# Spectral filter and leaky feed-forward in one kernel: first layer begun with two token groups, 8-byte runs from the first transposes, and a new plan for the later batches

## The chip, the cores and the metric

The kernel runs on one core of one Trainium2 chip. The metric is the device time of one execution in microseconds (us). Before the change four executions took 754.4 to 758.41 us, with a median of 756.79. Lower is better.

## The reference

The input `x` holds 8 batches of 3008 tokens of 256 features. Along the tokens of each batch a real Fourier transform is taken, multiplied with a complex filter, and transformed back. Then every one of the 24064 tokens goes through two matrix products with a leaky ReLU between them.

```python
X = np.fft.rfft(x, axis=1)                       # x: (8, 3008, 256)
Y = X * (filt_r + 1j * filt_i)[None, :, :]
y = np.fft.irfft(Y, n=3008, axis=1)
h = y.reshape(24064, 256) @ w_in                 # 256 -> 2048
out = np.maximum(0.01 * h, h) @ w_out            # 2048 -> 256, float32
```

## The kernel before, in words

**The transform.** 3008 is 94 times 32, so a transform of one batch is four small matrix stages with a turn of the layout between the first and the second pair. For a batch `b` these are: `s1` (line 219, 16 groups of one matmul, over the 94), `s2` (line 265, 12 groups of two matmuls, over the 32), the filter, `sa` (line 285, 12 groups of one matmul, back over the 32), and `sb` (line 303, 16 groups of four matmuls, back over the 94), which writes the tokens' features into `yt`. A group of `s1` fills one PSUM bank and is copied to SBUF by VectorE (DVE) or ScalarE (ACT), line 222. Two groups together are stored to a DRAM buffer `dz1` (line 224, 256 KB) and, when all eight stores have landed, read back turned, six reads of 256 KB, of which `z1` holds four (line 229). `sa` does the same through `dz2` and `z2`: stores at line 289, reads at line 234, copies at line 287.

**The filter.** For one `s2` group DVE multiplies the bank with the two parts of the filter (lines 274 and 277; for the even groups of batch 1 the exchange of real and imaginary halves is done by two half-width multiplications, lines 271 and 272). For the others two DMAs (lines 275, 276) exchange the halves in SBUF. GpSimd (POOL) adds (line 279); the sum is what `sa` reads.

**Batch 0** takes another way, without DRAM: `first_s1`, four DVE transposes (line 255), `first_s2` (line 328; ACT copies at line 336 and POOL multiplications at line 339 take some of its groups), `first_sa` (line 349), four more DVE transposes (line 357), and `first_sb` (line 366, 16 groups of eight matmuls, groups 0 to 7 for the first 128 features and 8 to 15 for the last 128; each group is copied to `yt` at line 295). Nothing of the feed-forward runs before all 16 are issued.

**The feed-forward** works on 47 chunks of 512 tokens. `moe1` (line 442, 32 matmuls of 512 columns for a chunk, more where a chunk crosses two batches) fills pairs of banks `ph`, which ACT takes through the leaky ReLU (line 447, 1024 columns at a time). The second product of chunks 0 to 3 and of the last is plain (line 545, 64 matmuls of 256 columns; results are copied at line 550). For the chunks between, seven half-size products (line 493, 112 matmuls of 128 columns) stand for eight; they need four sums of 2048 columns on DVE (line 470, `act_sums`), and one DVE or ACT instruction that takes each product out of its bank (lines 517 to 537).

**The order** is written by hand. A heap `work` holds closures with a planned time; they are run in order of time, and what they call is recorded in that order on each engine's queue. Each engine then works through its own queue strictly in order, held only by semaphores. The planned unit is an eighth of a chunk: chunk `ci` of `moe1` is spread over times 8 ci to 8 ci + 8, its second product over the eight units after that. `plan(b, ...)` gives each batch a start and a step for `s1`, `s2`, `sa` and `sb`; two groups are never nearer than `GAP` = 0.6 units. Planned times decide the order only.

All DMAs of `dz1`, `dz2`, the exchange and the output are issued by SyncE (SP), from one queue: an issue that waits for its data holds up all issues behind it. The loads of `x` are issued by POOL.

**Banks.** Until the first layer begins the transform stages use three single banks `pf` and two double ones `ph`. From there two `pf` banks are left for `s1`, `s2`, `sa` and `sb` in turn, and the third and `po_ps` serve the second product.

The lines that set the order around the change, before:

```python
t1_part(0, 0, True)(), t1_part(0, 1, True)()            # 390, writes flat
for g in range(8, 16):                                  # 420
    first_sb(g, act if g in (10, 12, 14) else dve, two[(g // 2) % 2])
plan(1, 0.3, 0.55, 12.8, 1.25, 3.3, 37, 2.8, 4, 1.6)    # 575
plan(2, 13, 1.55, 43.5, 2.6, 5.5, 84.2, 2.8, 13, 2.3)
plan(3, 42, 1.75, 75, 3.75, 6, 129, 2.94, 4, 2.94)
after = when[stage, b, 15 if stage == 1 else 11] + LANDED      # 591
at(max(time, after, place.get((stage, c % 4), 0)), f)
```

Of the kernel before, what the change touches and what calls it, by code (L numbers as in the profile page):

```python
# [73 lines left out]
def kernel(  # L74
# [25 lines left out]
    LANDED = 1.7  # L100
    SUMS = (0.9, 1.9, 2.9, 3.9)
# [45 lines left out]
    def at(time, f):  # L147
        clock["n"] += 1
        heapq.heappush(work, (time, clock["n"], f))

# [63 lines left out]
    st1, st2, st1_more = ring(big[2], 0), ring(big[2], 1), ring(big[0], 0)  # L214

    def s1_group(b, g, copy):
        def go():
            ps = bank("pf", 2, D)
            nc.tensor.matmul(ps, fwd1[:N1], x_sb[:N1, ds(2 * g, 2), :], start=True, stop=True)  # L219
            h = g // 2  # L220
            st = st1[h % 4] if b > 1 or h < 4 else st1_more[h % 4]
            copy(st[:, ds(2 * (g % 2), 2), :], ps)  # L222
            if g % 2:
                soon(0.7, lambda: nc.sync.dma_start(dz1[b % 2][ds(4 * h, 4)].rearrange("n p d -> p n d"), st))
        return go

    def t1_load(b, c):
        def go():
            nc.sync.dma_start(z1[c % 4], turned(dz1[b % 2], N2, c))
        return go  # L230

    def t2_load(b, h):
        def go():
            nc.sync.dma_start(z2[h % 4][:K4], turned(dz2[b % 2], NC, h))
        return go
# [11 lines left out]
    def t1_part(b, i, flat=False):  # L247
        def go():
            a = big[(4 * b) % 3][:].bitcast(FP32)[:, ts(i, E4 * Q)].rearrange("p (e n) -> p e n", n=Q)
            o = big[(4 * b + 1) % 3][:].bitcast(FP32)  # L250
            if flat:
                o = o[:, ts(i, E4 * Q)].rearrange("p (e n) -> p e n", n=Q)
            else:
                o = o.rearrange("p (n e) -> p e n", n=Q)[:, ts(i, E4), :]
            nc.vector.transpose(o, a)
        return go


    ys = {}

    def s2_group(b, g):
        def go():
            ps = bank("pf", 2, D)
            for j in range(2):
                nc.tensor.matmul(ps[:, j, :], f2_sb[:, 2 * g + j, :],  # L265
                                 z1[g // 2 % 4][:, 2 * (g % 2) + j, :],
                                 start=True, stop=True)
            fa, fb = fa_sb[:, ds(2 * g, 2), :], fb_sb[:, ds(2 * g, 2), :]
            p1, p2, p3 = (scrp.tile([P, 2, D], FP32, tag=f"p{i}", name=f"p{i}_b{b}_g{g}") for i in (1, 2, 3))
            if b == 1 and g % 2 == EXG:  # L270
                nc.vector.tensor_tensor(p3[0:64], ps[64:P], fb[64:P], AL.mult)
                nc.vector.tensor_tensor(p3[64:P], ps[0:64], fb[0:64], AL.mult)
            else:
                nc.vector.tensor_tensor(p2[:], ps, fb, AL.mult)  # L274
                soon(1, lambda: nc.sync.dma_start(p3[0:64], p2[64:P]))
                soon(1, lambda: nc.sync.dma_start(p3[64:P], p2[0:64]))
            nc.vector.tensor_tensor(p1[:], ps, fa, AL.mult)  # L277
            ys[(b, g)] = y1 = ypp.tile([P, 2, D], FP16, tag="y", name=f"y_b{b}_g{g}")
            soon(1.2 if b == 1 and g % 2 == EXG else 3 if b > 1 else 2.6, lambda: nc.gpsimd.tensor_tensor(y1[:], p1[:], p3[:], AL.add))  # L279
        return go  # L280

    def sa_group(b, g):
        def go():
            ps = bank("pf", 2, D)
            nc.tensor.matmul(ps, inv2, ys.pop((b, g))[:], start=True, stop=True)  # L285
            h = g // 2
            nc.scalar.copy(st2[h % 4][:, ds(2 * (g % 2), 2), :], ps)  # L287
            if g % 2:
                soon(0.7, lambda: nc.sync.dma_start(dz2[b % 2][ds(4 * h, 4)].rearrange("k p d -> p k d"), st2[h % 4]))
        return go  # L290
# [6 lines left out]
    def sb_group(b, g, copy):  # L297
        h, dt = g // 2, g % 2

        def go():  # L300
            ps = bank("pf", 4, N1)
            for j in range(4):
# [21 lines left out]
    def first_s2(hf, c, n, kind, on_pool=False):  # L324
        ps = bank(kind, n, DH)
        src = paired(big[1])
        for j in range(n):
            nc.tensor.matmul(ps[:, j, :].rearrange("p (e t) -> p e t", t=2), f2_sb[:, c + j, :],
                             src[:, c + j, ts(hf, DH // 2)], start=True, stop=True)
# [29 lines left out]
    def first_sb(g, copy, kind):  # L359
        dt, h = g // 8, g % 8  # L360
        src = big[0][:].rearrange("p (h n e r t) -> p h n r t e", h=2, n=Q // 2, r=2, t=2)
# [28 lines left out]
    t1_part(0, 0, True)(), t1_part(0, 1, True)()  # L390
    upper(0, fa_sb, act), upper(0, fb_sb, minus)
    first_s2(0, 8, 8, "ph", True)
    t1_part(0, 2, True)()
# [7 lines left out]
    t1_part(0, 3, True)()  # L401
# [18 lines left out]
    for g in range(8, 16):  # L420
        first_sb(g, act if g in (10, 12, 14) else dve, two[(g // 2) % 2])
# [44 lines left out]
    def act_sums(ci, step):  # L466
# [3 lines left out]
        nc.vector.tensor_tensor(o, i0, i1, op)  # L470

# [15 lines left out]
    def product(ci, a, w, after):  # L487
# [4 lines left out]
        def one(t, c):  # L492
            nc.tensor.matmul(po[:, t], a()[:, c, ts(t, P)], w[:, c, :],  # L493
# [21 lines left out]
    def last_product(ci):  # L515
        def after(po):
            add(rows(ci, 0)[:, :, 1], po, rows(ci, 1)[:, :, 2], AL.add)
            soon(0.5, lambda: stores(ci, 0))
        return product(ci, lambda: s4, b22, after)

    def products(ci):
        a11, a12, a21, a22 = (lambda i=i, j=j: quarter(ci, i, j) for i in range(2) for j in range(2))

        def after5(po):
            add(rows(ci, 1)[:, :, 1:3], twice(po), part[1], AL.add)
            soon(0.5, lambda: stores(ci, 1))
# [8 lines left out]
        items += product(ci, a21, wt[2], lambda po: add(v7, po, t1, AL.add))  # L535
        items += product(ci, lambda: s2, wt[1], lambda po: add(part[1], twice(po), part[0], AL.add))
        items += product(ci, a22, wt[3], lambda po: add(rows(ci, 1)[:, :, 0], po, u3, AL.add))
        items += product(ci, lambda: s1, wt[0], after5)
        return items

    def plain(ci):

        def one(tj, ct):
# [7 lines left out]
            soon(0.5, lambda: store(ci, tj, ot[:]))  # L551
        return [lambda tj=tj, ct=ct: one(tj, ct) for tj in range(4) for ct in range(NCT)]

    groups, loads = [], []

    def plan(b, s1, s1_step, s2, s2_step, lag, sb, sb_step, xl, x_step):
        for g in range(16):
            groups.append((s1 + s1_step * g, 1, b, g, s1_group(b, g, dve if b == 1 and g % 4 < 3 else act)))
            if g % 2 and b + 1 < B:
                at(s1 + xl + x_step * g, lambda n0=2 * g - 2: x_load(b + 1, n0, 4))  # L560
        for c in range(6):
            loads.append((s2 - 3, 1, b, c, t1_load(b, c)))
# [3 lines left out]
        for h in range(8):  # L566
            loads.append((sb - 3, 3, b, h, t2_load(b, h)))
        for g in range(16):
            due = SL * (QT * (8 * b + g // 2) // CH)
            groups.append((min(sb + sb_step * g, due - 3.5 + 2 * (g % 2)), 4, b, g, sb_group(b, g, act)))  # L570
# [3 lines left out]
    at(26, lambda: nc.sync.dma_start(i1_sb[:K4], i1t_d.ap()))  # L574
    plan(1, 0.3, 0.55, 12.8, 1.25, 3.3, 37, 2.8, 4, 1.6)
    plan(2, 13, 1.55, 43.5, 2.6, 5.5, 84.2, 2.8, 13, 2.3)
    plan(3, 42, 1.75, 75, 3.75, 6, 129, 2.94, 4, 2.94)
    for b in range(4, B):
        z = 47 * b
        plan(b, z - 121, 2.94, z - 69, 3.92, 6.5, z - 11.6, 2.94, 4, 2.94)  # L580

    last, when = -1, {}
    for time, stage, b, g, f in sorted(groups, key=lambda v: v[0]):
        last = max(time, last + GAP)
        when[stage, b, g] = last
        at(last, f)
        assert stage < 4 or last < SL * (QT * (8 * b + g // 2) // CH), (b, g, last)
    place = {}
    for time, stage, b, c, f in loads:

        after = when[stage, b, 15 if stage == 1 else 11] + LANDED
        at(max(time, after, place.get((stage, c % 4), 0)), f)
        place[stage, c % 4] = when[stage + 1, b, 2 * c + 1] + 0.1
# [49 lines left out]
```

## Time and profile before

| What | Value |
|---|---|
| four executions | 756.01, 757.56, 754.4, 758.41 us |
| the profiled execution | 756.01 us, of which its span is 754.2 us |
| TensorE (PE) busy | 739.3 us, 98% of the span |
| ACT, DVE, POOL busy | 562.4, 484.6, 165.1 us |
| granted TensorE clock | 1.00 in every stretch of 20 us but the last (0.99) |
| first matmul of the feed-forward | 38.16 us |
| start of the last merged row of matmuls (16 of 256 columns) | 748.93 us |
| bytes moved by DMA | 113.29 MB, 150 GB/s on average |

Times in the profile count from the start of the span. A row of the timeline merges equal instructions that follow each other: its start, its length, the engine, the line, the operation, the tiles, partitions and columns, the count, and in brackets the idle time before it with what ended it. Matmuls are pipelined and their ends are modelled, so a row's length is longer than the time for which it holds PE; the distance from the start of one row to the start of the next is what the next one really waited.

### The profile page before, as it was taken

The page shows a single profiled execution, that of the slowest core. Times are in us where ns is not written, and L with a number is a line of the kernel's source. Part 1 is how long each engine was busy: PE and PEld are TensorE (multiplying, and loading weights), DVE is VectorE, ACT ScalarE, POOL GpSimd, SP SyncE. Part 2 cuts the span into 40 slices and gives each one's busy share as a digit, 9 for nine tenths or more (in the row PEclk, how much of TensorE's full clock was granted, in tenths as well). Part 3 has the DMA queues.
Part 4 walks back from the last instruction along what each step waited for, and adds up shares of the span by engine and source line. Part 5 has one row for each costly group of instructions (what it writes and reads, how often), then busy time and mean ns, then how long its engine had stood idle before and what let it go on. Part 6 is the DMA issues. An engine that isn't in the chain of part 4 may idle for free.

```text
span 754.2 us, 18976 instructions
## 1 busy us (share of the span) xinstructions
PE 739.3 (98%) x7829; PEld 529.1 (70%) x7829; DVE 484.6 (64%) x658; ACT 562.4 (75%) x755; POOL 165.1 (22%) x171
## 2 busy tenths in 40 slices
PE   8899999999999999999999999999999999999998
PEld 4555657667777777877678767787777777777776
DVE  5965525777666785667666756676677676555462
ACT  4876777788778877777778777878777777776663
POOL 4702421332222122221223222213111210000000
PEclk9999999999999999999999999999999999999999
DMA  9997786887875667555765656553554433111012
GB/s 189 247 208 200 171 203 179 195 197 204 224 205 147 142 189 203 149 154 129 209 173 143 170 135 181 147 142 115 149 161 116 118 96 104 53 64 54 29 44 70
DMA packets 119687, 113.29 MB, mean 150 GB/s; under 512 B 16352, under 2 KB 92768, under 8 KB 119408
## 3 DMA queue, kind: packets, MB, share of 16 engines
q1 hardware_dynamic: 104736, 95.59, 42.3%
q0 software_dynamic: 14864, 16.49, 15.4%
q8 instruction: 61, 1.00, 0.6%
q14 instruction: 26, 0.21, 0.1%
HBM read 57.48 MB, written 50.33 MB: 143 GB/s over the span
## 4 chain that ended last, share of the span: by engine, by line
PE 83%; DMA 3%; DVE 1%; ACT 0%; issue 0%; POOL 0%; SPq 0%; DVEq 0%; POOLq 0%; ACTq 0%
PE ph L442 38%; PE pf L493 17%; PE po_ps L493 17%; PE pf L303 3%; PE pf L219 2%; PE pf L285 2%; PE pf L265 2%; DMA big<-dz 1%; PE pf L545 1%; PE po_ps L545 1%; DMA p_b_g<-p_b_g 1%; DVE big L470 1%; DMA dz<-big 1%; DVE p_b_g L277 0%; POOL y_b_g L279 0%
## 5 line engine op out<-in xcount | busy, mean ns | idle before, releaser
L447 ACT ACTIVATE gt_c<-ph 128x1024 f16<-128x1024 f32 x376 | 385.1, 1024 | 138.0 <-PE ph L442 129.2
L442 PE MATMUL ph<-yt,w_in_sb 128*128 128x512 f16 (+7 forms) x1728 | 447.2, 351 | 0.1
L493 PEld LDWEIGHTS <-gt_c 128*128 128x128 f16 x2688 | 194.3, 98 | 89.5 <-issue 0.7
L279 POOL TENSOR_TENSOR y_b_g<-p_b_g,p_b_g 128x512 f16<-128x512 f32 x84 | 114.1, 1360 | 442.3 <-DMA p_b_g<-p_b_g 327.5
L493 PEld LDWEIGHTS <-big 128*128 128x128 f16 x2016 | 144.8, 98 | 62.2 <-issue 1.4
L442 PEld LDWEIGHTS <-w_in_sb 128*128 128x128 f16 x1728 | 138.1, 98 | 19.5 <-issue 0.8
L274 DVE TENSOR_TENSOR p_b_g<-pf,fb_sb 128x512 f32<-128x512 f32 x78 | 53.8, 690 | 50.6 <-PE pf L265 32.3
L222 ACT CAST big<-pf 128x512 f16<-128x512 f32 x100 | 58.2, 583 | 13.5 <-PE pf L219 12.4
L493 PE MATMUL pf<-wt_sb,gt_c 128*128 128x128 f16 x672 | 67.5, 219 | 0.0
L493 PE MATMUL po_ps<-wt_sb,gt_c 128*128 128x128 f16 x672 | 67.4, 219 | 0.0
L493 PE MATMUL po_ps<-wt_sb,big 128*128 128x128 f16 x672 | 64.8, 219 | 0.0
L493 PE MATMUL pf<-wt_sb,big 128*128 128x128 f16 x672 | 64.0, 219 | 0.0
L493 PE MATMUL po_ps<-w_out_sb,gt_c 128*128 128x128 f16 x672 | 64.0, 219 | 0.0
L493 PE MATMUL pf<-w_out_sb,gt_c 128*128 128x128 f16 x672 | 63.5, 219 | 0.1
L295 ACT CAST yt<-pf 128x376 f16<-128x376 f32 x117 | 55.1, 473 | 8.6 <-PE pf L303 6.0
L277 DVE TENSOR_TENSOR p_b_g<-pf,fa_sb 128x512 f32<-128x512 f32 x84 | 57.3, 682 | 0.2
L470 DVE TENSOR_TENSOR gt_c<-gt_c 128x2048 f16<-128x2048 f16 x42 | 54.5, 1297 | 1.1
L287 ACT CAST big<-pf 128x512 f16<-128x512 f32 x84 | 49.1, 584 | 8.1 <-PE pf L285 6.9
L470 DVE TENSOR_TENSOR big<-gt_c,big 128x2048 f16<-128x2048 f16 x42 | 54.6, 1300 | 0.0
L470 DVE TENSOR_TENSOR big<-gt_c 128x2048 f16<-128x2048 f16 x42 | 53.8, 1280 | 0.2 <-ACT gt_c L447 0.2
L470 DVE TENSOR_TENSOR big<-big,gt_c 128x2048 f16<-128x2048 f16 x42 | 53.3, 1269 | 0.0
L219 PE MATMUL pf<-x_sb,small_sb 94*128 94x512 f16 x112 | 42.7, 381 | 1.4 <-DVE p_b_g L277 1.3
(84 smaller groups left out, 640.2 us busy)
## 6 DMA issues: line engine op xcount, KB each, us to landing
dz<-big SPq DMA_DIRECT2D x98, 256.0 KB
p_b_g<-p_b_g SPq DMA_DIRECT2D x156, 128.0 KB
out_dram<-ost_c_h SPq DMA_DIRECT2D x114, 128.0 KB
big<-dz SPq DMA_DIRECT2D x42, 256.0 KB
big<-dz SPq DMA_DIRECT2D x56, 192.0 KB
x_sb<-in_x_dram POOLq DMA_DIRECT2D x41, 192.0 KB, 4.4
out_dram<-ost_c_t SPq DMA_DIRECT2D x14, 128.0 KB
x_sb<-in_x_dram POOLq DMA_DIRECT2D x2, 768.0 KB, 10.3
```

The source lines that it names most:

```text
L219: nc.tensor.matmul(ps, fwd1[:N1], x_sb[:N1, ds(2 * g, 2), :], start=True, stop=True)
L222: copy(st[:, ds(2 * (g % 2), 2), :], ps)
L274: nc.vector.tensor_tensor(p2[:], ps, fb, AL.mult)
L277: nc.vector.tensor_tensor(p1[:], ps, fa, AL.mult)
L279: soon(1.2 if b == 1 and g % 2 == EXG else 3 if b > 1 else 2.6, lambda: nc.gpsimd.tensor_tensor(y1[:], p1[:], p3[:], AL.add))
L287: nc.scalar.copy(st2[h % 4][:, ds(2 * (g % 2), 2), :], ps)
L295: copy(yv, ps.rearrange("p c a -> p a c"))
L303: nc.tensor.matmul(ps[:, j, :], z2[h % 4][:K4, j, ts(dt, P)], i1_sb[:K4, 4 * h + j, :], start=True, stop=True)
L442: nc.tensor.matmul(ph[:, j, ds(t - ci * CH, e - t)], w_in_sb[:, dt, ts(ct, P)], yt[:, dt, ds(t % N, e - t)], start=(dt == 0), stop=(dt == ...
L447: nc.scalar.activation(gts[ci][:, ds(2 * g, 2), :], ph, AF.Lrelu)
L470: nc.vector.tensor_tensor(o, i0, i1, op)
L493: nc.tensor.matmul(po[:, t], a()[:, c, ts(t, P)], w[:, c, :], start=(c == 0), stop=(c == NCH - 1))
```

## The change

- The first transposes write runs of 8 bytes: pairs of neighbouring `n` stand side by side, and `first_s2` reads them so (stride 8 bytes in place of 128).
- Only groups 0 to 9 of `first_sb` stand before the first layer. Groups 10 to 15 are put into the first layer's stream at the planned times `REST`, copied by ACT and DVE in turn.
- The second half of batch 1's staging moves from `big[0]` to `big[1]`, since `big[0]` is still read.
- `place` of a group: a group of `s2` or `sb` is planned no earlier than its read-back's issue, and a group of `sa` behind its POOL addition.
- All starts, steps and delays have new values, those of DVE's four sums (`SUMS`) too; a read-back is issued `LEAD` before its first use, where the stores allow it.

```diff
-    LANDED = 1.7
-    SUMS = (0.9, 1.9, 2.9, 3.9)
+    LANDED = 2.26
+    SUMS = (0.05, 1.51, 3.08, 4.47)
+    REST = (7.21, 11.38, 12.49, 9.32, 22.05, 21.68)
+    DUE = (3.63, 2.48)
+    LEAD = (3.88, 6.29)
+    AFTER = (0.72, 0.81, 2.69, 4.11, 0.05, 0.67)
+    PLANS = (
+        (0.68, 0.17, 11.96, 1.17, 4.08, 36.48, 2.68, 4.72, 1.5),
+        (11.42, 1.71, 43.45, 2.46, 6.81, 87.35, 2.71, 14.75, 1.96),
+        (39.96, 1.78, 73.73, 3.9, 6, 128.81, 2.82, 0.75, 2.65),
+        (63.05, 2.86, 119, 3.9, 7.12, 177.38, 3.11, 10.44, 2.21),
+    )
...
-    st1, st2, st1_more = ring(big[2], 0), ring(big[2], 1), ring(big[0], 0)
+    st1, st2, st1_more = ring(big[2], 0), ring(big[2], 1), ring(big[1], 1)
...
+    def first_t1(i):
+        a = big[0][:].bitcast(FP32)[:, ts(i, E4 * Q)].rearrange("p (e n r) -> p e n r", n=Q // 2, r=2)
+        o = big[1][:].bitcast(FP32).rearrange("p (n e r) -> p e n r", n=Q // 2, r=2)
+        nc.vector.transpose(o[:, ts(i, E4)], a)
+
+    def y_delay(b, g):
+        return 1.2 if b == 1 and g % 2 == EXG else AFTER[2] if b > 1 else AFTER[3]
...
-        src = paired(big[1])
+        src = big[1][:].rearrange("p (n e r t) -> p n r e t", n=Q // 2, r=2, t=2)
...
-    for g in range(8, 16):
-        first_sb(g, act if g in (10, 12, 14) else dve, two[(g // 2) % 2])
+    for g in (8, 9):
+        first_sb(g, (act, dve)[g % 2], "ph")
...
+    for g in range(10, 16):
+        at(REST[g - 10], lambda g=g: first_sb(g, (act, dve)[g % 2], "pf"))
...
+    def load_time(stage, b, c):
+        end = stage, b, 15 if stage == 1 else 11
+        if (stage, b, c) not in loads:
+            if end not in when or (c > 3 and (stage + 1, b, 2 * c - 7) not in when):
+                return None
+            loads[stage, b, c] = t = max(first_use[stage, b] - LEAD[stage // 2], place.get((stage, c % 4), 0),
+                                         when[end] + AFTER[4 * (stage // 2)] + LANDED)
+            at(t, (t1_load if stage == 1 else t2_load)(b, c))
+        return loads[stage, b, c]
...
+        if stage == 3:
+            behind = when[2, b, g] + y_delay(b, g) + 0.02 if (2, b, g) in when else None
+        else:
+            behind = load_time(stage - 1, b, g // 2) if stage != 1 else 0
+        if behind is None or behind + 0.02 > t:
+            heapq.heappush(queue, (t + GAP if behind is None else behind + 0.03, n, stage, b, g, f))
+            continue
+        when[stage, b, g] = last = t
+        at(t, f)
```

`AFTER` holds the delays from a copy to its `dz1` store, from the multiplication to the exchange, from it to POOL's addition (later batches, then the odd groups of batch 1), from a copy to its `dz2` store, and to an output store; before these were 0.7, 1, 3, 2.6, 0.7 and 0.5. `need` and `noted`, which the change also adds, only check the recorded order while the program is built. Batches 5 to 7 take the last line of `PLANS`, moved by 47 units each. The matmuls are the same before and after, 7829 of them; of the copies of `first_sb` one goes from DVE to ACT.

## The prediction

> **What bounds the kernel.** The first page says PE is busy for 739.3 of 754.2 us, but ends of matmuls are modelled, so I read PE's timeline from start to start. Back to back, a matmul of 512 columns holds PE for 0.216 us, one of 256 for 0.109, one of 128 for 0.056, one of `sb` for 0.045 (rows of 2 x 512 start 0.43 apart, 16 x 256 take 1.75, 16 x 128 0.89, 4 of `sb` 0.18). From the first matmul of the feed-forward (38.16) to the end of the last (748.93 + 1.75 = 750.7) are 712.5 us. The work in them is: `moe1` 1728 matmuls 325.3, the halved products 4704 x 0.056 = 263, plain ones 320 x 0.109 = 35, `s1` and `sa` 196 x 0.216 = 42.3, `s2` 168 x 0.109 = 18.4, `sb` 448 x 0.045 = 20.2; together 704.3. So PE sets the time, and some 8 us are waits. A change can win only these, and the start of the first layer. I then looked for each wait, as distance between starts less the work. Over 0.11 us they are: 1.75 at 56.9, 0.14 at 69.1, 0.33, 0.30, 0.30, 0.27, 0.17 between 74 and 100, 0.88 at 111.4, 1.47 at 142.1, 0.14 at 268.6, 0.58 at 365.3, 1.37 at 449.7, 0.12 at 499.8: **7.8 us**. Who ends them stands in the waits of PE (total, times, longest):
>
> ```profile
> PE pf L265 <- DMA big<-dz: 2.8, 2, 1.6
> PE ph L328 <- DVE big L255: 2.6, 2, 2.2
> PE pf L219 <- DVE p_b_g L277: 1.3, 1, 1.3
> ...
> PE pf L303 <- DMA big<-dz: 0.7, 1, 0.7
> ...
> PE pf L285 <- POOL y_b_g L279: 0.4, 1, 0.4
> ```
>
> Read-backs (L265, L303), one late filter product (L277), one late addition (L279). L328 lies in the prologue.
>
> **Start of the first layer.** Before, PE begins the second half of `first_sb` at 35.52, when the last transpose ends (33.09 + 2.37 = 35.46), and the first layer 2.64 later. After, only groups 8 and 9 stand there: two groups take PE 0.49 (rows of 16 start 0.49 apart). ACT's eight copies of groups 0 to 7 end at 35.46 + 0.92 = 36.38; group 8's (0.47) ends at 36.85, DVE copies group 9 beside it. So the first layer can start at 36.85: **-1.3**. The six groups come back as 48 matmuls x 0.031: **+1.5**.
>
> **First transposes.** The DVE rows L255 (flat, 1233 ns) and L357 (already 8-byte runs, 1223 ns) cost the same, so writing costs nothing. What changes is `first_s2`'s read:
>
> ```profile
> 17.21 1.92 PE L328 MATMUL ph<-big,f_sb 128*128 128x128 f16 x16 [0.41 <-DVE big L255]
> 18.95 1.06 PE L328 MATMUL pf<-big,f_sb 128*128 128x128 f16 x8
> ```
>
> 16 matmuls hold PE for 1.74, 0.109 each, where L493's of the same size need 0.056. With runs of 8 bytes the cost lies between 0.109 (no gain) and 0.056; nearest is L366, whose weights are read at that stride and hold no matmul up (0.031 each), so I take 0.056. The Trainium skill, "SBUF — State Buffer", section "Door 1: The DMA port swizzle", says full rate needs at least two hits in one 16-byte line: a stride of 128 bytes misses that, 8 bytes meets it; by it the gain below stands whole. The first eight matmuls then end 0.44 earlier. ACT's copy (18.29, free since 17.66), POOL's chain from 18.95, and the last `first_sa` follow: PE waits there 0.44 for POOL's L339, DVE 0.77 for ACT's copy before 33.09. So the last transposes end up to 0.44 earlier: **-0.45**, bounds -0.45 and 0. DVE covers the rest (18.05 of 20 us busy in 20 to 40).
>
> **Collisions in the first layer.** I set the recorded order of PE beside the row lengths. A bank needs about 1.15 us from one group's start to its reuse (start to copy 0.42, copy 0.69). `s1` groups 10 and 11 of batch 1 start 0.89 apart in one bank, with a `first_sb` group in the other, whose copy waits behind ACT's 1.02 us. **+0.5**; bounds 0 and 1.0. The copies themselves (three of 0.47 on ACT, three of 0.54 on DVE) lie beside PE's work: from 40 to 60 ACT is busy for 14.5 of 20 us, DVE for 11.0. The load of the later `i1_sb` has to wait for the last of the six, 40 us into the first layer by PE's work, and is first read at 70. `big[1]`, where batch 1 now stages, is last read by `first_s2` (25.68 + 1.04), long before 38.
>
> **First read-back of batch 1.** The longest wait before:
>
> ```profile
> 50.96 0.38 PE L219 MATMUL pf<-x_sb,small_sb 94*128 94x512 f16 x1
> ...
> 56.93 0.49 PE L545 MATMUL po_ps<-w_out_sb,gt_c 128*128 128x256 f16 x3
> 59.00 0.38 PE L265 MATMUL pf<-big,f_sb 128*128 128x256 f16 x2 [1.58 <-DMA big<-dz]
> ```
>
> with SP's queue beside it:
>
> ```profile
> 52.81 0.69 SPq L482 DMA_DIRECT2D out_dram<-ost_c_t  x1
> 55.91 1.76 SPq L229 DMA_DIRECT2D big<-dz  x4
> ```
>
> From `s1` group 15 to data is 7.82 us (copy to 51.95, store landed 55.9, read landed 59.0), and PE has 6.1 us of work between. After, there are 5.9 us of work between, group 15's copy stands behind an activation (0.5 later), and SP has two output stores ahead of the read. The second waits for the chunk's second result, whose last matmul ends 4.2 us behind group 15; 0.2 to DVE, 0.42 copy, 0.6 issue give 5.4, and 3.1 to the landing 8.5. So the wait becomes 8.5 - 5.9 = **2.5**, 0.75 more than before; bounds 1.5 and 3.5.
>
> A rule that speaks against a longer wait here: the Trainium skill, "TensorE: Matmul & The Clock Gate", says PE falls to half clock after about an idle window of 3.4 us. The trace shows 2.2 us idle before 23.05 and 1.58 before 59.00 with the granted clock at 1.00; by the rule, a wait past 3.4 us would cost one more window at half clock, 1.7 us (an estimate from that page). My sum leaves it out.
>
> **Second read-back of batch 1** (0.88 before): it needed 5.74 + 0.88 = 6.6 us after the copy of `sa` group 11, and the new order has 6.9 us of work there: **-0.9**. Bounds -0.9 and 0.
>
> **Filter of batch 1.** Five waits (0.17 to 0.33, sum 1.4) come where an even group holds its bank for three DVE products (0.2 + 3 x 0.69 = 2.3) with 2.2 us to the reuse. The new order has such pairs at groups 0, 2 and 10 only: three of 0.3, **-0.5**. All `sa` of this batch get more room (7.3 to 12.9 us after `s2` against 6.1 to 10).
>
> **Sums.** The 1.47 at 142 is DVE's: two sums stand in front of a filter product.
>
> ```profile
> 140.06 2.31 DVE L470 TENSOR_TENSOR big<-gt_c,big 128x2048 f16<-128x2048 f16 x1
> 142.30 0.68 DVE L274 TENSOR_TENSOR p_b_g<-pf,fb_sb 128x512 f32<-128x512 f32 x1
> 142.90 0.68 DVE L277 TENSOR_TENSOR p_b_g<-pf,fa_sb 128x512 f32<-128x512 f32 x1
> ```
>
> The sums were one unit apart and are now about 1.45. Walking DVE's queue with the rows' means, before has two groups late (the one at 142 among them), after has none, the tightest just in time: **-1.5**. Bounds -1.5 and +1.0 (a sum of 2.31 instead of 1.29 at the tightest place).
>
> **Late waits.** At 365 an exchange took 5.5 us, at 450 a read-back 7.05 us from its issue at 444.24, where the plan leaves 3 units (5.6 us) for it. The new lead is 3.88 units (7.3 us) for `s2` and more for `sb`; PE work from `s1` group 15 to `s2` rises from 14 to 23 to 26 us for batches 4 to 7, and from `s2` to `sa` from 11.8 to 12.6. **-1.95**; bounds -1.95 and 0. Batch 2's `s2` has less (10.4 against 11.3 us), batch 3's `sb` too (10.6 against 13.2), so I add **+0.3** for new ones, bounds 0 and 2. Other moved DMAs (loads of `x`, `dz2` stores issued at once) wait in SP or POOL, behind no read-back that is due.
>
> **Sum:** -1.3 + 1.5 - 0.45 + 0.5 + 0.75 - 0.9 - 0.5 - 1.5 - 1.95 + 0.3 = **-3.6**. Against the profiled execution (756.0; span 754.2 and 1.8 around it) that is **752.4**. The median of four is 0.8 higher, so against it the same 752.4 is 4.4 less. About 0.5%, 3.8 us, is what a measurement of this kernel can tell from no change: below 753.0 counts as faster, above 760.6 as slower.
>
> **Rivals.**
> - *Waits only move* (0.21): the read-back of batch 1 takes its upper bound (+1.0), `first_s2` stays at 0.109 (+0.45), 365 and 450 come back elsewhere (+1.5 of 1.95): 755.4. For it: the first DMAs are at 1.0 to 1.5 of their share from 38 to 52 us, and the exchange's time swings. Against: more room nearly everywhere. That the 8-byte runs do nothing is part of it.
> - *More is won* (0.17): the read-back meets its lower bound (-1.0), no collision (-0.5), no new wait (-0.3): 750.6, or down to 749.5 if executions like the slower ones before (758.4) lose more waits than the profiled one shows.
> - *The first sum blocks DVE* (0.07, slower). At 0.05 units into a chunk it stands at DVE's head until ACT's last activation ends. In my walk 25 later `s2` groups have under 1.0 us to spare. If the first sum ends a full 1.0 us later each time (2.31 instead of 1.29), they lose together 10.5 us: 752.4 + 10.5 = 762.9. Under 0.5 us late it costs 2.3 at most and doesn't decide. Only 0.2 us of waiting for ACT at L470 speaks for it before.
>
> **Chances.** Forecast 0.55, of which 0.35 falls below 753.0. Faster 0.35 + 0.17 = 0.52; same 0.20 + 0.21 = 0.41; slower 0.07. The range 749.5 to 756.5 takes in the forecast, the first rival and most of the second.
>
> **What would show it.** First `moe1` near 36.4; `first_s2` at 0.056 each; a wait near 2.5 us at batch 1's first `s2`, none at its first `sb`; none over 0.5 us after 130. I am wrong if DVE's L277 or a read-back ends long waits there, or if the first wait passes 3.5.

## The result, and the profile after

The changed kernel takes 758.47 us (median; 755.79 to 763.0), the kernel before 757.12 beside it: a ratio of 1.0025, 95% interval 1.0017 to 1.0033. It is slightly slower, where 752.4 and a gain of 3.6 us were forecast. The profiled execution took 759.25 us with a span of 757.5, 3.3 more than that of before. It lies 0.8 us above its kernel's median and the one before 1.1 us below its own, so the two profiles differ by more than the 0.25% (1.9 us) of the kernels. Lines are numbered by the changed kernel from here on: `first_s2` is L361, `s1` L244, `s2` L293, `sa` L315, `sb` L336, `moe1` L477, a read of `dz1` L256, an output store L518, POOL's addition L308.

The waits of PE, changed kernel (total, times, longest):

```profile
PE ph L361 <- DVE big L280: 3.8, 2, 3.4
PE pf L293 <- DMA big<-dz: 3.0, 1, 3.0
PE pf L315 <- POOL y_b_g L308: 1.2, 1, 1.2
...
PE pf L336 <- DMA big<-dz: 0.4, 1, 0.4
```

The late filter product is gone, and one read-back less is waited for. But the first read-back takes 3.0 us in place of 1.6, an addition of POOL 1.2 (at 200 us) in place of 0.4, and the wait in the prologue has grown from 2.2 to 3.4. Where that comes from, PE's timeline shows:

```profile
17.27 1.07 PE L361 MATMUL ph<-big,f_sb 128*128 128x128 f16 x16 [0.41 <-DVE big L280]
18.18 0.61 PE L361 MATMUL pf<-big,f_sb 128*128 128x128 f16 x8
18.64 1.02 PE L413 MATMUL po_ps<-idle 128*128 128x512 f16 x4
23.08 1.89 PE L361 MATMUL ph<-big,f_sb 128*128 128x128 f16 x16 [3.42 <-DVE big L280]
```

16 matmuls of `first_s2` now hold PE for 0.91 us, 0.057 each, as forecast. PE is done sooner, and the next transpose comes when it came before (23.08, before 23.05): DVE sets it. So the gain became idle time, and the same 16 matmuls then took 1.69 us (23.08 to 24.77). The reason stands in the granted clock. Stretches of 3.41 us of the changed kernel; the columns are the busy time of PE, weight loads, DVE, ACT and POOL, then PEclk (1.00 is full speed, 0.50 half), the share of the DMA engines and GB/s:

```profile
18.78:22.19 3.41, 0.88 (x5) 0.19 (x2) 3.41 (x5) 2.95 (x3) 3.41 (x4) 1.00 1.70 196
22.19:25.60 3.41, 2.52 (x18) 1.99 (x19) 3.38 (x4) 1.58 (x3) 3.41 (x4) 0.50 1.06 228
25.60:29.01 3.41, 3.41 (x15) 1.76 (x14) 3.38 (x4) 1.81 (x3) 3.40 (x4) 0.50 1.08 318
...
59.74:63.15 3.41, 0.51 (x5) 0.49 (x6) 0.02 (x1) 0.73 (x1) 0.00 (x0) 1.00 0.78 234
63.15:66.56 3.41, 3.41 (x13) 1.69 (x12) 2.05 (x3) 0.91 (x2) 1.23 (x1) 0.50 0.21 78
66.56:69.97 3.41, 3.41 (x26) 2.36 (x25) 3.00 (x5) 1.85 (x3) 0.03 (x1) 1.00 0.50 147
```

The clock is at half speed from 22.19 to 29.01 and from 63.15 to 66.56 (called the half clock from here on), each time behind a stretch in which PE worked for under 1 us. Both begin on one grid: 63.15 - 22.19 = 12 x 3.413. The second follows the wait for the first read-back. That wait, in the changed kernel's SP queue and on PE:

```profile
54.37 0.36 SPq L249 DMA_DIRECT2D dz<-big  x1
54.82 3.86 SPq L518 DMA_DIRECT2D out_dram<-ost_c_t  x2
58.89 1.86 SPq L256 DMA_DIRECT2D big<-dz  x4
```

```profile
62.65 0.38 PE L293 MATMUL pf<-big,f_sb 128*128 128x256 f16 x2 [3.01 <-DMA big<-dz]
```

The read stands behind the second of two output stores, which is issued at 58.12, once DVE has copied its result (0.42 us from 57.67).

From the first `moe1` to the end, the sum by starts of rows, before and after: first `moe1` 38.16 and 38.00 (-0.2); six groups of `first_sb` inside (+1.5); first read-back 1.75 and 3.18 (+1.4); second 0.88 and 0 (-0.9); half clock from 63.15 (+1.2 to 1.7); chunk 0, which takes 11.12 us in place of 10.29, 0.2 of it one group (+0.6, of which 0.3 stands ahead of 39.16, where the first `moe1` waits for DVE's copy of group 9, done at 38.46, and some 0.3 at the collision between 46.9 and 47.8); filter of batch 1 1.4 and 0.33 (-1.1); the wait at 142 (-1.5); those at 365, 450 and 500 (-2.1); new ones of 0.39 at 155, 1.36 at 200, 0.54 at 210, 0.48 at 289 and 0.25 at 596 (+3.0). That is +1.9 to 2.4 of the 3.2 us by which the last matmul is later (its row starts at 751.97; before, at 748.76, not at the 748.93 of the table); some 1 us is spread over waits too short for this list.

### The profile page after: what moved, and what is told of

It is laid out like the page before. It is cut to its first block, busy times and chain, and to the rows that moved or that the text cites. A ratio compares the mean times of both kernels' runs of the same rounds, so it can differ in the third digit from the quotient of the medians.

```text
span 757.5 us, 18982 instructions
## 1 busy us (share of the span) xinstructions
PE 741.3 (98%) x7829; PEld 529.0 (70%) x7829; DVE 482.8 (64%) x657; ACT 564.2 (74%) x756; POOL 164.1 (22%) x171
## 4 chain that ended last, share of the span: by engine, by line
PE 93%; DMA 2%; DVE 2%; issue 1%; SPq 1%; ACT 1%; POOL 0%; DVEq 0%; POOLq 0%
PE ph L477 42%; PE pf L531 17%; PE po_ps L531 17%; PE pf L244 3%; PE pf L336 3%; PE pf L293 2%; PE pf L315 2%; PE po_ps L583 2%; PE pf L583 2%; DMA big<-dz 1%; DMA x_sb<-in_x_dram 1%; PE pf L382 1%; DVE big L280 1%; PE ph L361 1%; SPq L518 0%
## 5 line engine op out<-in xcount | busy, mean ns | idle before, releaser
L477 PE MATMUL ph<-yt,w_in_sb 128*128 128x512 f16 (+7 forms) x1728 | 448.2, 352 | 0.3 <-ACT yt L326 0.2
L531 PEld LDWEIGHTS <-gt_c 128*128 128x128 f16 x2688 | 195.1, 98 | 89.6 <-issue 1.8
L308 POOL TENSOR_TENSOR y_b_g<-p_b_g,p_b_g 128x512 f16<-128x512 f32 x84 | 113.4, 1350 | 423.6 <-DMA p_b_g<-p_b_g 245.3
L477 PEld LDWEIGHTS <-w_in_sb 128*128 128x128 f16 x1728 | 137.7, 98 | 19.7 <-issue 1.2
L505 DVE TENSOR_TENSOR big<-gt_c 128x2048 f16<-128x2048 f16 x42 | 55.4, 1319 | 0.4 <-ACT gt_c L482 0.2
L505 DVE TENSOR_TENSOR gt_c<-gt_c 128x2048 f16<-128x2048 f16 x42 | 52.6, 1252 | 0.8
L583 PEld LDWEIGHTS <-gt_c 128*128 128x128 f16 x320 | 31.6, 99 | 18.6 <-issue 1.1
```

What stands on the lines that cost most here:

```text
L308: ("y", b, g), lambda: nc.gpsimd.tensor_tensor(y1[:], p1[:], p3[:], AL.add)))
L477: nc.tensor.matmul(ph[:, j, ds(t - ci * CH, e - t)], w_in_sb[:, dt, ts(ct, P)], yt[:, dt, ds(t % N, e - t)], start=(dt == 0), stop=(dt == ...
L583: nc.tensor.matmul(po, gts[ci][:, ct, ts(tj, P)], w_out_sb[:, ct, :], start=(ct == 0), stop=(ct == NCT - 1))
```

## Experiments on the start: clock and 8-byte runs

My theory: PE's longer idle time halves the clock, which makes the first layer late, and the long first read-back does it again. The rival: the plan of the later batches and its new waits cost the time, and the clock is covered by other engines. All ratios are against the kernel before on the same chip, with 95% intervals; the changed kernel stands at 1.0025 (1.0017 to 1.0033).

**e1_warm**, idle matmuls over the gap:

```diff
-    keep_warm(4)
+    keep_warm(14)
     first_s2(1, 8, 8, "ph", True)
```

> The changed kernel with 14 idle matmuls (in place of 4) behind the first half of first_s2. They cover 10 x 0.216 = 2.2 us of the 3.42 us in which PE waits for the transposes before 23.08. Theory A (the wait halves the clock, and the half clock makes the first layer late): granted clock 1.00 from 22 to 30 us, first moe1 at 36.4 to 37.0 in place of 38.00, time 1.0 to 1.6 us below the changed kernel. Rival B (PE at half clock is covered by DVE and ACT in the prologue; the loss lies behind the first layer's start): the clock is 1.00 too, but the first moe1 stays within 0.3 us of 38.0, and so does the time.

Measured: 1.0032 (1.0014 to 1.0051). The clock stays at 1.00 from 20 to 38 us and the first `moe1` comes at 37.49, not below 37. And then:

```profile
34.65:38.06 3.41, 2.30 (x42) 1.81 (x39) 1.78 (x3) 2.63 (x7) 0.00 (x0) 1.00 1.04 197
38.06:41.48 3.42, 3.42 (x9) 1.22 (x9) 0.98 (x2) 1.02 (x1) 0.03 (x1) 0.50 1.44 198
```

The half clock came 16 us later, in chunk 0, which took 12.82 us in place of 11.12: 1.70 more, half of 3.41. Ahead of it, PE has little but `first_sb` (the 2.30 is from modelled ends: by starts, two rows of 0.49 and a few matmuls, some 1.3). So the change's early start itself leaves PE idle enough for it. Theory A is right on what a half-clock stretch costs PE and wrong on the gain: the time is that of the changed kernel.

**e2_flat** takes the 8-byte runs out of the changed kernel:

```diff
-        a = big[0][:].bitcast(FP32)[:, ts(i, E4 * Q)].rearrange("p (e n r) -> p e n r", n=Q // 2, r=2)
-        o = big[1][:].bitcast(FP32).rearrange("p (n e r) -> p e n r", n=Q // 2, r=2)
-        nc.vector.transpose(o[:, ts(i, E4)], a)
+        a = big[0][:].bitcast(FP32)[:, ts(i, E4 * Q)].rearrange("p (e n) -> p e n", n=Q)
+        o = big[1][:].bitcast(FP32)[:, ts(i, E4 * Q)].rearrange("p (e n) -> p e n", n=Q)
+        nc.vector.transpose(o, a)
...
-        src = big[1][:].rearrange("p (n e r t) -> p n r e t", n=Q // 2, r=2, t=2)
+        src = paired(big[1])
...
-                             src[:, (c + j) // 2, (c + j) % 2, ts(hf, DH // 2)], start=True, stop=True)
+                             src[:, c + j, ts(hf, DH // 2)], start=True, stop=True)
```

> The changed kernel with the flat first transposes of before, and first_s2 reading them at a stride of 128 bytes. Theory A: first_s2 goes back to 0.109 us a matmul, PE's wait before 23 us to 2.2 us, the clock stays at 1.00, first moe1 at 36.8 to 37.2, time 0.6 to 1.2 us below the changed kernel: the 8-byte runs cost where they were to gain. Rival B (8-byte runs gain what they should): first moe1 0.3 to 0.5 us later than 38.0, time up by as much.

Measured: 1.0023 (1.0004 to 1.0042), the same as the changed kernel. `first_s2` is back at 0.109. PE idled 2.46 us and the clock was halved all the same, from 23.70 to 27.11:

```profile
23.64 1.92 PE L361 MATMUL ph<-big,f_sb 128*128 128x128 f16 x16 [2.46 <-DVE big L280]
```

Both expectations miss: the 8-byte runs show neither a cost nor a gain here, within an interval of 0.2% either way, and 3.4 us of idling is not needed.

**e3_only8**, the same runs alone in the kernel before (the edit of e2_flat turned round, there):

> The kernel before with the 8-byte runs alone. Theory A: PE waits 3.4 us before 23 us, granted clock 0.5 from 23 to 29 us, first moe1 at 38.5 to 39.8 in place of 38.16, time 0.4 to 1.6 us above the kernel before. Rival B: first moe1 0 to 0.45 us earlier than 38.16, time 0 to 0.45 us below.

Measured: 0.9997 (0.9981 to 1.0013). PE idles 3.54 us, the clock is halved from 23.22 to 26.63, the first `moe1` comes at 38.74, 0.6 later, and the last matmul ends 0.5 later than in the profiled execution of before; the medians show no difference. What happens to the prologue is as A says; that it costs the execution as much isn't shown.

## Experiments on the read-backs

**e4_read** issues the first four reads of batch 1 ahead of the second output store; no instruction of another engine moves:

```diff
-            at(t, (t1_load if stage == 1 else t2_load)(b, c))
+            at(t - (0.2 if (stage, b) == (1, 1) and c < 4 else 0), (t1_load if stage == 1 else t2_load)(b, c))
```

> The changed kernel with the first four read-backs of batch 1 put into SP's queue ahead of the second output store of chunk 0, and no other instruction moved on any engine. Theory A: the read-back lands some 2.5 us earlier, PE's wait for it falls from 3.0 to 0.4 to 1.0 us, no stretch at half clock follows at 63 to 67 us, time 3 to 4 us below the changed kernel (2.2 of the wait and 1.5 of the half clock). Rival B (the half clock here is covered): 2.0 to 2.4 us below. Rival C (the store is not what holds the read, the stores to dz1 are): no change within 0.5 us.

Measured: 0.9978 (0.9962 to 0.9994), 0.47% or 3.6 us below the changed kernel, though the half clock still came from 24.43 and from 38.08. SP's queue and PE, e4_read:

```profile
56.00 0.69 SPq L518 DMA_DIRECT2D out_dram<-ost_c_t  x1
57.90 2.82 SPq L256 DMA_DIRECT2D big<-dz  x4
60.76 0.56 SPq L518 DMA_DIRECT2D out_dram<-ost_c_t  x1
```

```profile
61.03 0.38 PE L293 MATMUL pf<-big,f_sb 128*128 128x256 f16 x2 [0.22 <-DMA big<-dz]
```

The wait is 0.22 in place of 3.01 and no half clock follows. A holds and C falls; B's 2.0 to 2.4 us is at the edge of what the two intervals allow (some 2.2 to 4.9 us), so the gain of the wait is shown and its split between wait and clock is not. The place in SP's queue is the largest single loss of the change.

**e12_plan** keeps only the plan: flat transposes as in e2_flat, and

```diff
-    for g in (8, 9):
-        first_sb(g, (act, dve)[g % 2], "ph")
+    for g in range(8, 16):
+        first_sb(g, act if g in (10, 12, 14) else dve, two[(g // 2) % 2])
...
-    for g in range(10, 16):
-        at(REST[g - 10], lambda g=g: first_sb(g, (act, dve)[g % 2], "pf"))
```

> The changed kernel with the front of before: flat first transposes, all 16 groups of first_sb ahead of the first layer. Only the new plan of the later batches, the delays and the places of the read-backs are left. The prediction's terms for these sum to -3.8 us (0.75 - 0.9 - 0.5 - 1.5 - 1.95 + 0.3). Theory A (the read-back behind the output store and the waits of batch 3 near 200 us eat what the plan wins): first read-back's wait 2.5 to 3.2 us, waits for L308 near 200 us of 1 to 3 us, time within 1.5 us of the kernel before. Rival B (the loss lies in the front alone): 2 to 4 us below the kernel before.

Measured: 1.0017 (0.9999 to 1.0035). A holds: the plan alone, forecast at -3.8 us, gains nothing. Its first read-back was waited for 3.41 us, L308 for 2.17 at 209.57, and both halved the clock (60.76 to 67.59, and here):

```profile
207.54:210.95 3.41, 1.38 (x17) 1.02 (x17) 0.86 (x1) 1.34 (x2) 1.68 (x1) 1.00 0.79 227
210.95:214.36 3.41, 3.41 (x24) 2.25 (x22) 0.42 (x1) 1.50 (x2) 1.75 (x2) 0.50 0.81 223
```

A wait of 2.2 us is enough, where it lies in one stretch of the grid.

**e5_lag** adds to e4_read a longer way from `s2` to `sa` for batch 3. The wait at 200 us in the changed kernel:

```profile
193.19 2.38 SPq L518 DMA_DIRECT2D out_dram<-ost_c_h  x3
195.68 0.53 SPq L303 DMA_DIRECT2D p_b_g<-p_b_g  x1
```

```profile
201.93 0.38 PE L315 MATMUL pf<-y_b_g,small_sb 128*128 128x512 f16 x1 [1.21 <-POOL y_b_g L308]
```

Its `s2` stands at 190.78, DVE's product is ready at 191.95, but the exchange is issued at 195.68, behind three output stores, and lands 4.9 us later. The new rule put this `s2` 1.5 units behind its planned time (75.22 in place of 73.73) and left its `sa` at 80.02.

```diff
-        (39.96, 1.78, 73.73, 3.9, 6, 128.81, 2.82, 0.75, 2.65),
+        (39.96, 1.78, 73.73, 3.9, 7.5, 128.81, 2.82, 0.75, 2.65),
```

> e4_read with batch 3's sa planned 7.5 units behind its s2 in place of 6 (its s2 was pushed back 1.5 units by the rule that puts groups behind their read-backs, its sa was not). Theory A (the waits for POOL's L308 near 200 and 207 us come from this lost lag): no wait over 0.3 us for L308 there, time 1.2 to 2.5 us below e4_read's 755.8. Rival B (SP's queue makes the exchange as late wherever the sa stands): the waits stay at 1 us or more, time within 0.5 us of e4_read.

Measured: 0.9956 (0.9938 to 0.9973) from six executions, below both kernels. No wait for L308 of 0.2 us or more is left; one of 0.69 for the read-back of batch 2 at 205 is. A holds for the waits; the 0.2% below e4_read are not clear of noise, since the two intervals overlap.

**e14_lag_same_chip** is e5_lag beside e13_minus_warm (below):

> e5_lag once more, on one chip with e13_minus_warm, since its interval rests on few executions and e10_warmpad, without a stretch at half clock up to 60 us, was no faster. Theory A (each stretch at half clock costs up to 1.7 us to the end): its executions with a granted clock of 0.995 to 0.996 are 1.5 us or more slower than those at 0.998 to 1.000, and its median is 0.8 to 1.6 us above e13_minus_warm. Rival C: its executions differ by under 0.8 us between these clocks, and its median is within 0.5 us of e13_minus_warm.

Measured: 0.9963 (0.9949 to 0.9978). Its four executions at a granted clock of 0.995 took 754.9 us on average, the five at 0.998 to 1.000 754.5, and its median is 0.9 us below that of e13_minus_warm. Theory A falls: to take the stretches away gains nothing. Rival C holds for the clocks and misses for the medians (0.5). That a stretch costs nothing isn't shown: with the three at 0.997 counted in, the eight faster-clocked executions take 754.1, in e5_lag it is 755.4 (3 at 0.995) against 754.1 (3), in e11_minus 755.3 (6) against 753.9 (6).

## Experiments on DVE, POOL and ACT in the prologue

With the 8-byte runs, DVE's `minus` on the second half of the imaginary filter takes 1.76 to 2.01 us in place of 1.19 beside POOL's products, wherever it stays on DVE (e6_port and e8_all, 5.2, apart); in e2_flat it takes 0.95. The kernel before and the changed kernel:

```profile
24.20 1.19 DVE L374 TENSOR_SCALAR fb_sb<-fb_sb 64x3072 f16<-64x3072 f16 x1
```

```profile
24.23 1.91 DVE L408 TENSOR_SCALAR fb_sb<-fb_sb 64x3072 f16<-64x3072 f16 x1
```

**e6_port**, on e4_read:

```diff
-    first_s2(0, 16, 4, "pf", True)
     for n0 in (0, N2 // 2):
         x_load(1, n0, N2 // 2)
+    first_s2(0, 16, 4, "pf", True)
```

> e4_read with batch 1's loads of x issued on POOL ahead of the two products of the third part of first_s2 (c = 16), no other order changed. In the kernel before, DVE's minus at 24.20 took 1.19 us while POOL's product beside it took 1.87; with the 8-byte runs POOL's product starts some 0.3 us earlier, takes 1.15, and DVE's minus 1.8 to 2.0. Theory A (the two take turns, first come first served, and DVE sets the end of the prologue): with POOL's product later, the minus takes 1.2 again, the last transposes start 0.4 to 0.7 us earlier than 33.48, first moe1 at 36.8 to 37.1 in place of 37.50, time 0.4 to 0.8 us below e4_read. Rival B (the minus is slow for another reason, the reads of x or fb): it stays at 1.8 to 2.0, nothing moves.

Measured: 1.0019 (1.0003 to 1.0035), first `moe1` at 41.43. POOL and DVE of e6_port:

```profile
24.27 1.17 POOL L372 TENSOR_TENSOR prod<-fx_h_c,fa_sb 128x512 f16<-128x512 f32 x1
25.39 1.16 POOL L372 TENSOR_TENSOR prod<-fx_h_c,fb_sb 128x512 f16<-128x512 f32 x1
26.51 2.27 POOL L372 TENSOR_TENSOR prod<-fx_h_c,fa_sb 128x512 f16<-128x512 f32 x2
29.68 2.27 POOL L372 TENSOR_TENSOR prod<-fx_h_c,fb_sb 128x512 f16<-128x512 f32 x2 [0.91 <-DVE fb_sb L408]
```

```profile
24.39 5.21 DVE L408 TENSOR_SCALAR fb_sb<-fb_sb 64x3072 f16<-64x3072 f16 x1
```

Both of my expectations fall. The `minus`, ready 0.12 us after a product had started, ended at 29.60; since it takes 0.95 alone and POOL stood idle from 28.77 to 29.68, waiting for it, it ran only from about 28.75 by my reading: four products back to back kept it out. In e4_read the issues of `x_load` stood behind the second product and gave it a gap. In the kernel before it came in between two products all the same (at 24.55); why there and not here stays open. So the shared access is there, but not by turns. The Trainium skill, "SBUF — State Buffer", section "Who interferes with whom", says that a `tensor_scalar` of DVE can take the port pair that it shares with GpSimd, and that the later one blocks until the first is done; here it was blocked through four instructions.

**e11_minus**, on e5_lag:

```diff
-    upper(1, fb_sb, minus)
+    upper(1, fb_sb, lambda o, i: nc.scalar.mul(o, i, -1.0))
```

> e5_lag with the negation of the second half of the imaginary filter on ACT in place of DVE, so that POOL's products can't hold it up (in e6_port they held it for 5.21 us, in e4_read for 1.87). Theory A (DVE sets the end of the prologue, and the hold is shared port time of DVE and POOL): DVE's products start at once, the first moe1 comes 0.9 to 1.9 us earlier than 37.52, time lower by as much. Rival B (ACT is late then, its copy takes some 2.75 us): first moe1 within 0.4 us of 37.5 or later, time the same or up to 1 us more.

Measured: 0.9962 (0.9947 to 0.9977), as e5_lag. DVE's products start at once (24.48), but the first `moe1` stays at 37.52: ACT's 2.76 us from 22.71 make its copies for POOL late (25.50 in place of 23.99 in e6_port), and PE was at half clock from 24.38 to 27.79. Rival B on the time; which of the two held it, e13_minus_warm tells.

## Experiments on what the half clock costs

**e7_warm2**, on e4_read:

```diff
-    keep_warm(4)
+    keep_warm(14)
     first_s2(1, 8, 8, "ph", True)
...
+    keep_warm(4)
     for g in (8, 9):
         first_sb(g, (act, dve)[g % 2], "ph")
+    keep_warm(2)
```

> e4_read with idle matmuls in every gap of PE up to the first layer: 14 in place of 4 ahead of the second half of first_s2, 4 ahead of groups 8 and 9 of first_sb, 2 behind them. In all traces so far the granted clock is at half speed for stretches of 3.41 us or twice that, at multiples of 3.41 us from each other, each behind a stretch in which PE had idled for some 2 us or more. Theory A (these stretches cost half of their length where PE sets the pace, and the gaps call for them): no half clock from 20 to 60 us, chunk 0 takes 11.1 us from first moe1 to first plain product in place of 12.8, mean granted clock of the executions over 0.998, time 1.2 to 1.9 us below e4_read. Rival B (the half clock has another cause than idling, or costs nothing): it comes in as many executions, time within 0.5 us of e4_read.

Measured: 1.0002 (0.9987 to 1.0017). The clock did what A says: none halved from 20 to 60 us, chunk 0 in 10.96 us, a mean granted clock of 0.9992 over the executions (e4_read 0.9961). The time did not, it is 0.24% above e4_read's, which neither theory expected: the last `s1` store was issued 1.5 us earlier than in e4_read (54.01, 55.55), but it landed 4.17 us after its issue in place of 2.35, PE waited 2.12 us for the read-back, and then the clock was halved from 62.67 to 66.09.

**e8_all**, the edits of e5_lag, e6_port and e7_warm2 together:

> e4_read with the edits of e5_lag, e6_port and e7_warm2 together. Theory A: the three gains add, 2.8 to 5.2 us below e4_read, so 750.6 to 753.0 us, below the kernel before. Rival B: what is won early is waited for later (read-backs of batch 1 hold the pace), at most 1.5 us below e4_read.

Measured: 1.0039 (1.0021 to 1.0057). e6_port's loss is in it (first `moe1` at 41.50), and the store landed after 3.94 us. It is some 4.6 us above e4_read, so both expectations miss, and nothing is told apart by it but that these two losses stay.

**e9_pad** asks why the store landed late, on e5_lag:

```diff
+    def tiny(n):
+        for _ in range(n):
+            nc.tensor.matmul(po_ps[:, 0, 0:16], idle[:, 0:P], idle[:, 0:16], start=True, stop=True)
...
     keep_warm(4)
+    tiny(16)
     first_s2(1, 8, 8, "ph", True)
```

> e5_lag with 16 idle matmuls of 16 columns (0.5 us in all) in PE's gap before 23 us, nothing else. In every trace an instruction load of 16 KB (DMA queue q8) holds one of the 16 DMA engines for some 1.7 us between 52 and 62 us, and its place goes with PE's instruction count. Where it fell behind the issue of batch 1's last store to dz1 (the kernel before, e7_warm2, e8_all), that store landed 3.9 to 4.2 us after its issue; where it did not (e3_only8, e4_read, e5_lag, e6_port), 2.3 to 2.7 us. Theory A: the 32 instructions more move it into the store, which lands 3.7 to 4.3 us after its issue, PE waits 1.5 to 2.3 us for the first read-back in place of 0.3, time 1 to 2.5 us above e5_lag's 754.55. Rival B (the landing swings by itself): 2.3 to 2.7 us as in e5_lag, time the same within 0.5 us.

Measured: 0.9992 (0.9973 to 1.001). The last store and the read behind it in SP's queue, and the DMA queues from 53.8 to 57.5 us (packets, MB, share of 16 engines), e9_pad:

```profile
53.83 0.36 SPq L249 DMA_DIRECT2D dz<-big  x1
...
57.42 1.76 SPq L256 DMA_DIRECT2D big<-dz  x4
```

```profile
q8 instruction: 1, 0.02, 2.0%
```

The instruction load fell to 54.4, the store landed 3.59 us after its issue (e5_lag: 2.36), just short of A's 3.7, and PE waited 1.54 us for the read (e5_lag: 0.3). 2.0% of 16 engines in 3.7 us is 1.2 us of one engine. A holds for the landing and the wait. 16 idle matmuls, 0.5 us in an idle gap, cost 0.36% against e5_lag, which ran on another chip, and 0.3% against e11_minus on the same one; the profile shows 1.2 us of it in this wait and waits of 0.88 and 1.39 us at 100 and 114.

**e10_warmpad** puts both together, on e5_lag: the edit of e7_warm2, and e9_pad's 16 small matmuls behind its `keep_warm(14)`.

> e5_lag with the idle matmuls of e7_warm2 and 16 small ones more, which move the instruction load ahead of the issue of the last store. Theory A: no half clock from 20 to 60 us, the store lands 2.3 to 2.8 us after its issue, the wait for the first read-back is under 0.9 us, first s2 at 59.4 to 60.2 in place of 60.95, time 0.8 to 1.9 us below e5_lag. Rival B (the read-back has another anchor, and what the clock gives is waited away): first s2 at 60.9 to 61.5, time within 0.5 us of e5_lag or above it.

Measured: 0.9977 (0.9962 to 0.9992). All steps of A came: no half clock, the instruction load at 53.0 ahead of the store, landing after 2.35, `s2` at 59.68. But the time is no lower than e5_lag's. The 1.27 us won at `s2` are 0.50 at the first `sb` (111.33, e5_lag 111.83) and 0.30 at the end; PE waits 1.37 us for batch 2's read-back in place of 0.69, and the two stand level. The rows of e5_lag and of e10_warmpad:

```profile
205.88 0.35 PE L336 MATMUL pf<-i_sb,big 96*128 96x94 f16 x4 [0.69 <-DMA big<-dz]
```

```profile
205.85 0.35 PE L336 MATMUL pf<-i_sb,big 96*128 96x94 f16 x4 [1.37 <-DMA big<-dz]
```

Here time won ahead of the read-backs of batches 1 and 2 was waited away, by PE for DMA.

**e13_minus_warm** is e10_warmpad with e11_minus's edit:

> e10_warmpad (no stretch at half clock, instruction load ahead of the store) with the negation on ACT of e11_minus. Theory A (in e11_minus the first layer came no earlier because the half clock from 24.4 to 27.8 us held PE's first_s2 and first_sa; the prologue is DVE's, then PE's): first moe1 at 36.3 to 37.0 in place of 37.52 and 37.97, first s2 at 58.2 to 59.2, time 0.8 to 1.6 us below e5_lag of this same call. Rival B (ACT's 2.76 us for the negation makes ACT the bound of the prologue): first moe1 at 37.3 to 37.9. Rival C (PE's gain early on is waited away by the read-backs of batches 1 and 2): first moe1 early, but the time within 0.5 us of e5_lag.

Measured: 0.9981 (0.9963 to 0.9998). Without half clock the first `moe1` comes at 37.43: rival B, ACT holds the prologue then (DVE waits 1.06 us for its copy before the last transposes). `s2` stands at 59.09, 0.8 earlier than in e14_lag_same_chip, and yet the median is 0.9 us higher (755.25 and 754.37). Theory A falls, and rival C has the direction: nothing is gained. Where it goes isn't shown by this pair: the profiled execution of e14_lag_same_chip is the slowest of its twelve (756.9 us), and beside it the lead of 0.8 at `s2` even grows to 1.4 by 266. The pair of e5_lag and e10_warmpad above is the one that shows such a lead being waited away.

## Why the prediction was wrong, step by step

Three steps failed: the start of the first layer (-1.75 forecast, -0.2 measured), the half clock behind the first read-back, which the sum left out (+1.2 to 1.7), and the new waits of the later batches (+0.3 forecast, +3.0 measured).

- **Start of the first layer** (-1.3 and -0.45): failed. The first `moe1` came at 38.00, not 36.4; at full clock it comes at 37.49. Of these 1.1 us, 0.85 are the last transposes, which start at 33.50 and not at 32.65 since DVE's `minus` is held up by POOL, and 0.2 are group 8, which waits for ACT to free its bank (PE at 36.48). The half clock takes 0.5 more. And "DVE copies group 9 beside it" left out that this copy ends 0.5 us behind ACT's, at 38.46, which holds the first `moe1` up for 0.3. The step "the last transposes end up to 0.44 earlier", with "DVE covers the rest", named the engine that sets the end and gave the gain to another.
- **`first_s2` at 0.056**: right (0.057, and 0.109 again in e2_flat at a stride of 128 bytes), which agrees with the rule of the Trainium skill, "SBUF — State Buffer", section "Door 1: The DMA port swizzle". It gains nothing, since DVE paces it.
- **Collisions** (+0.5, bounds 0 and 1.0): chunk 0 lost 0.6, close to the term, but by luck: half of it is the copy of group 9; the collision itself cost some 0.3.
- **First read-back** (2.5, bounds 1.5 to 3.5): the mechanism was right, the size 3.0 to 3.2, inside the bounds. From the end of the last `s1` matmul (53.08) to data were 9.6 us, not 8.5. What failed is "my sum leaves it out": the half clock behind the wait. `s2` to the first `sb` took 52.27 us, and 51.05 in e1_warm, where no half clock followed: 1.2. e4_read shows wait and clock together as 3.6 us (2.2 to 4.9 by the intervals).
- **The clock gate.** The rule was weighed with the wrong bound. The Trainium skill, "TensorE: Matmul & The Clock Gate", section "What's actually happening", says that the window is free-running; the traces agree, with a grid of 3.41 us. So a wait need not pass 3.4 us. Waits of 2.1 to 3.4 us halved the clock where they fell into one window (0.51, 0.80, 0.88 and 1.38 us of work in it did, 1.61 did not), and waits as long can go free: 2.93 in e1_warm, split over two windows, and the 2.2 us before 23.05 in the kernel before. Where in the grid a wait falls differs between executions, so this cost is in part chance.
- **Second read-back** (-0.9): right in the changed kernel's profile, perhaps by luck. With the first wait mended it is back in some, 0 to 1.7 us (0.63 in e4_read, none in e5_lag). That the long first wait hid it isn't shown, since e2_flat and e12_plan wait 0.6 and 0.5 us here behind first waits of 2.7 and 3.4.
- **Filter** (-0.5), **sums** (-1.5), **late waits** (-1.95): right; -1.1, -1.5 and -2.1. The rival of the first sum blocking DVE did not come: no wait for DVE behind 130 us was over 0.5 us.
- **New waits** (+0.3, bounds 0 to 2): failed; 3.0. I compared PE's work between the stages by averages for the later batches and did not follow each exchange through SP's queue; three output stores stood ahead of batch 3's first. e5_lag takes that wait away; the 0.2% that it gains are not clear of noise.

With the two waits mended (e5_lag and e14_lag_same_chip, two numbers changed) the change is worth 0.4%, close to the 0.5% forecast. So the gain went into a queue, for the most part at the first read-back. That the total then comes near the forecast is in part luck: in e5_lag's profile the first `moe1` comes 0.6 us earlier than before, not 1.75, and the half clock costs chunk 0 another 1.7, while the first read-back is waited for 0.3 us, not 2.5.

What stays open: how much of the changed kernel's 0.25% is the half clock by itself. Its 54 executions have a mean granted clock of 0.9948 against 0.9973 to 0.9976 before; the six at 0.991 and 0.992 take 761.4 us on average, the fifteen at 0.997 and 0.998 757.7. But a long wait takes time and halves the clock at once, so these averages don't tell the two apart, and e10_warmpad and e13_minus_warm, which have almost no half clock (mean 0.9998 and 0.9996), are no faster than e5_lag and e14_lag_same_chip.

## What to carry to other kernels

When a queue issues stores and reads strictly in order, follow each read that something waits for to its place in the queue: one store ahead of it, which waited for another engine's result, cost 3.6 us here, most of the 4.7 us that the plan won on the filter, the sums and the late waits. An engine that becomes faster ahead of a wait wins only idle time, and in these traces idle time could halve the clock of the work behind it; so ask first which wait ends last there. And a rule with a threshold is to be read with its window: here 2.1 us of waiting were enough where they fell into one window of 3.41 us.

## What the runs showed of the hardware

- Half-clock stretches last 3.41 us or 6.82 us, start on a grid of 3.41 us that lies differently in each profiled execution, and cost PE half of their length where it sets the pace (1.70 us in chunk 0 of e1_warm).
- An instruction load of 16 KB held one DMA engine for 0.9 to 1.7 us; stores that it fell into landed 1.2 to 1.8 us later (3.6 to 4.2 us after their issue in place of 2.35). Idle instructions added to PE moved its place (e9_pad, e10_warmpad).
- DVE's `tensor_scalar` on 64 x 3072 halves took 0.95 us alone, 1.2 to 2.0 beside POOL's products, and 5.21 where these left no gap (e6_port).
